# A gated Fourier and Mish kernel: its hand-paced schedule is replaced by a list of operations sorted by when the matmul engine wants each

## The chip, the core and the metric

The kernel runs on one core of one Trainium2 chip. The metric is device microseconds of one execution, the median of timed runs. A core has the matmul engine TensorE (PE, with its weight loads PEld), VectorE (DVE), ScalarE (ACT), GpSimd (POOL) and SyncE (SP). Matmuls add into eight PSUM banks of 128 x 512 floats; ACT and DVE copy or add them out into SBUF tiles. DMAs carry tiles between SBUF and DRAM. Each engine works off its own queue in order, and instructions wait on semaphores.

## The reference

```python
x = A_x                                                  # 1 x 2048 x 640
g = sigmoid((x * gate_w).sum(-1, keepdims=True))
a = x @ dft_hid_re.T;  b = x @ dft_hid_im.T
A = dft_seq_re @ a - dft_seq_im @ b                      # Fourier mixing
h = x @ w1 + b1                                          # 640 -> 1728
B = (h * tanh(softplus(h))) @ w2                         # Mish, 1728 -> 640
out = g * A + (1 - g) * B
```

All is float32.

## The kernel before, in words

**Products.** Each float32 operand is split into a high part in PE's float32r format (a copy on ACT) and the rest (a subtraction on DVE): `split`, line 82. A product of two operands is three matmuls, `mm3` (line 91): high x high, high x low, low x high, each 128 x 128 weights by 128 x 512 columns.

**Stages.** Work is cut into tiles of 512 of the 2048 positions, two tiles to a "problem" (class `Problem`, line 293). Four problems multiply the sequence matrices by x (stage seq, results u), two multiply u by the hidden matrices (hid, results y), the dense part takes x by w1 and Mish (results act), and two problems take act by w2 and add y (out). u, y and act pass through DRAM scratch. Each problem is a 2 x 2 block product with seven products in place of eight (Winograd's form): sums and differences of the moving tiles (`s1` to `s4`) are made on DVE before their splits, and those of the weight blocks on DVE in jobs (`low`, `w1_job`). The 640 columns are four such blocks and a fifth, "block 5", that is multiplied plainly.

**Turns in a problem.** `first()` multiplies tile 11 by `a` (two banks) and by block 5 (`d1`). `second()` (line 343) goes through turns "22", "21", "s2", "s1"; "21" exists for block 5 of the second tile alone (`d2`, line 357). `third()` (line 452) goes through "12", "s3", "s4".

**The dense stage.** `dense_rest` does the columns of w1 that don't pair up. `dense_first` (line 734) goes through six blocks of w1 for each half of the positions. A block is eight steps on four banks (lines 863 to 870): a11 on bank a, s1 on b, d2 on d, s2 on a, s4 and d1 on b, s3 on a, a12 and d1 on c, a22 and d2 on a. Between two products on one bank, what it holds is copied out (`snap`) or added out (`add`).

**What sets the order.** `steps` (line 113) is the order of PE. The loop at lines 1040 to 1087 goes through it: for the step LEAD (7, or 6) ahead it issues the loads and splits; then the step's matmuls; then stores that are three steps old (`stores`, line 116, issued on SP); then what follows the step. Jobs (weight splits, the gate, products by g and 1 - g) start when a running sum of DVE's work is below that of PE (line 1079). All loads and stores are on SP's queue.

**The gate.** For each of four tiles, `gate` (line 885) multiplies five tiles of transposed x by columns of gate_w, splits the sum and multiplies it by a matrix of ones: two matmuls. g and 1 - g go to scratch as whole tiles. `gate_y` (line 919) loads each y again, multiplies it by g and stores it: 20 times.

**Buffers.** 20 tiles of 512 columns (f), 4 of 640 (fx), 10 operand pairs (rh, rl), 26 weight pairs of 640 columns (wh, wl).

Of the kernel before, what the change touches and what calls it, by code (L numbers as in the profile page):

```python
# [13 lines left out]
P = 128  # L14
# [8 lines left out]
LEAD = 7  # L23
LEAD_D = 6
AHEAD = 9
SPARE, SPARE_D, SPARE_OUT = 3, 5, 4
SLACK, SLACK_UP = -1.0, 2.5
NR, NFS, NFX, NW, NL = 10, 20, 4, 26, 4
MM = 0.2267


class Slots:


    def __init__(self, items):
        self.free = list(items)

    def get(self):
        return self.free.pop(0)

    def put(self, *items):
        self.free.extend(items)
# [3 lines left out]
def fnet_mish_gate(ctx: ExitStack, tc: tile.TileContext, xn, xt, c_re, c_im, wd_re, wd_im,  # L46
# [7 lines left out]
    psum = Slots([pp.tile([P, N], F32, name=f"ps{i}") for i in range(8)])  # L54
    R = Slots([(sb.tile([P, N], F32R, name=f"rh{i}"), sb.tile([P, N], F32R, name=f"rl{i}")) for i in range(NR)])
    FS = Slots([sb.tile([P, N], F32, name=f"f{i}") for i in range(NFS)])
    FX = Slots([sb.tile([P, D], F32, name=f"fx{i}") for i in range(NFX)])
    W = Slots([(sb.tile([P, D], F32R, name=f"wh{i}"), sb.tile([P, D], F32R, name=f"wl{i}")) for i in range(NW)])
    ones = sb.tile([P, P], F32R, name="ones")
    b1s = sb.tile([P, NF], F32, name="b1s")  # L60
    gws = sb.tile([P, KD], F32, name="gws")

    def scratch(name, n, rows=P):
        return [[dr.tile([rows, N], F32, name=f"{name}{i}_{t}") for t in range(TG)] for i in range(n)]

    usc, ysc = scratch("u", 2 * KD), scratch("y", KD)
    gsc, qsc = scratch("g", 1)[0], scratch("q", 1)[0]
    asc = scratch("act", FC) + [[dr.tile([FR, N], F32, name=f"actr_{t}") for t in range(TG)]]

    clock = {"pe": 0.0, "dve": 0.0, "step": 0}  # L70
# [4 lines left out]
    def tt(o, a, b, op):  # L75
        clock["dve"] += 0.14 + 0.54 * a.shape[-1] / N
        nc.vector.tensor_tensor(o, a, b, op=op)  # L77

    def copy(o, a, scale=1.0):
        nc.scalar.activation(o, a, AF.Copy, scale=scale)  # L80

    def split(h, l, src):

        copy(h, src)
        tt(l, src, f32(h), OP.subtract)

    def mm(ps, a, b, start, stop):
        clock["pe"] += MM
        nc.tensor.matmul(ps, a, b, start=start, stop=stop, skip_group_check=True)  # L89

    def mm3(ps, ah, al, bh, bl, start, stop):
        mm(ps, ah, bh, start, False)
        mm(ps, ah, bl, False, False)
        mm(ps, al, bh, False, stop)

    def part(w, a, b):
        return w[0][:, a:b], w[1][:, a:b]

    def blocks(w, at, n):
        return [part(w, at + j * P, at + (j + 1) * P) for j in range(n)]  # L100

    A2, B2 = slice(0, 2 * P), slice(2 * P, 4 * P)

    RAW, XS, PS, OPS, KEEP, X, H = {}, {}, {}, {}, {}, {}, {}
    steps, stores, events, attach, narrow, takes = [], [], {}, [], set(), {}

    def at(i, fn):

        events.setdefault(i, []).append(fn)

    def step(raw, preps, mms, post=None):
        steps.append([list(raw), list(preps), mms, post])

    def store(dst, v, f):
        stores.append((dst, v, f, clock["step"] + (3 if clock["step"] < len(steps) - 8 else 0)))


    jobs, loaded, running, done_jobs = [], [], [], set()  # L120

    class Job:
        def __init__(self, key, work, load=lambda: [], w=0, fx=0, fs=0):
            self.key, self.work, self.load, self.w, self.fx, self.fs = key, work, load, w, fx, fs

    def simple(fn):
        def work(*a):
            fn(*a)
            return
            yield  # L130
        return work

    def fx_load(src, width=D):
        f = FX.get()
        nc.sync.dma_start(f if width == D else f[:, :width], src)
        return f

    def fs_load(src):
        f = FS.get()
        nc.sync.dma_start(f[:src.shape[0]], src)  # L140
        return f

    def job_load(i):
        j = jobs.pop(0)
        loaded.append((j, j.load(), i))

    def job_start():
        j, a, _ = loaded.pop(0)
        running.append((j.key, j.work(*a)))

    def job_go():
        key, work = running[0]
        pause = next(work, None)
        if pause is None:
            running.pop()
            done_jobs.add(key)
        return pause or 0

    def need(key):
        while key not in done_jobs:  # L160
            if not running:
                if not loaded:
                    job_load(0)
                job_start()
            job_go()

    class Stage:  # L170


        def __init__(self, kind, kh, row, neg=False):
            self.kind, self.kh, self.row, self.neg = kind, kh, row, neg
            self.XA, self.XB, self.XT13 = [None] * kh, [None] * kh, [None] * kh
            self.XT2 = [None] * (kh // KD + 1)

    def t2_part(st, k):
        return part(st.XT2[k // KD], k % KD * P, (k % KD + 1) * P)

    def b_sums(f, g):

        t = FS.get()
        tt(f[:, A2], f[:, B2], f[:, A2], OP.subtract)
        tt(f[:, B2], g[:, B2], f[:, B2], OP.subtract)
        tt(t[:, A2], g[:, B2], f[:, A2], OP.subtract)
        tt(t[:, B2], g[:, A2], t[:, A2], OP.subtract)
        return t

    def top(st, k, a, five):  # L190
        w = st.XA[k] = st.XA[k] or W.get()
        split(*part(w, 0, 2 * P), a)
        split(*part(w, 2 * P, 3 * P), five)

    def low(st, k, g, f):
        if st.neg:
            copy(g, g, -1.0)
            yield 1
        t = b_sums(f, g)
        yield 0  # L200
        w = st.XB[k] = W.get()
        st.XA[k] = st.XA[k] or W.get()
        st.XT13[k] = W.get()
        if k % KD == 0:
            st.XT2[k // KD] = W.get()
        split(*w, g)
        FX.put(g)
        yield 0
        split(*part(st.XA[k], 3 * P, 5 * P), t[:, B2])
        split(*part(st.XT13[k], 4 * P, 5 * P), t[:, :P])  # L210
        split(*t2_part(st, k), t[:, P:2 * P])
        FS.put(t)
        yield 0
        split(*part(st.XT13[k], 0, 4 * P), f)
        FS.put(f)

    tops = set()

    def stage_jobs(st, order):
        def do_top(k, g):  # L220
            top(st, k, g[:, A2], g[:, 4 * P:])
            FX.put(g)

        for what, k in order:
            if what == "top":
                jobs.append(Job((st.kind, "top", k), simple(lambda g, k=k: do_top(k, g)),
                                lambda k=k: [fx_load(st.row(k))], (st.kind, k) not in tops, 1))
            else:
                jobs.append(Job((st.kind, "low", k), lambda g, f, k=k: low(st, k, g, f),
                                lambda k=k: [fx_load(st.row(k + st.kh)), fs_load(st.row(k)[:, :4 * P])],  # L230
                                2 + (k % KD == 0) + ((st.kind, k) not in tops), 1, 1))
            tops.add((st.kind, k))

    def c_split(key, f):
        r = OPS[key] = R.get()
        split(r[0], r[1], f)
        FS.put(f)

    def op_done(key):
        R.put(OPS.pop(key))  # L240

    def product(name, stationary, key, first, last):

        if first and name not in PS:
            PS[name] = [psum.get() for _ in stationary]
        for ps, w in zip(PS[name], stationary):
            mm3(ps, *w, *OPS[key], first, last)

    def products_by_part(uses, key):

        h, l = OPS[key]
        todo = []
        for name, stationary in uses:
            PS[name] = [psum.get() for _ in stationary]
            todo += zip(PS[name], stationary)
        for n, c in ((0, h), (0, l), (1, h)):
            for ps, w in todo:
                mm(ps, w[n], c, n == 0 and c is h, False)

    def free_banks(name):  # L260
        psum.put(*PS.pop(name))

    def copy_out(name, keep=False):
        f = [FS.get() for _ in PS[name]]
        for ps, o in zip(PS[name], f):
            copy(o, ps)
            if not keep:
                psum.put(ps)
        if not keep:
            PS.pop(name)  # L270
        return f

    def add_out(name, f, keep=False):

        for ps, a in zip(PS[name], f):
            tt(a, ps, a, OP.add)
        if not keep:
            free_banks(name)
        return f
# [853 lines left out]
```

## Time and profile before

| what | value |
|---|---|
| three timed runs | 885.54, 885.94, 887.34 us |
| median | 885.94 us |
| span of the profiled execution | 882.2 us |
| PE busy, matmuls | 864.0 us, 3780 |
| DVE busy, instructions | 724.2 us, 1262 |
| ACT busy, instructions | 477.5 us, 909 |
| DMA bytes, mean rate | 217.32 MB, 246 GB/s |

The span runs from the first to the last instruction of one execution; the median lies 3.7 us above it, and the time of that execution apart from its span isn't recorded. Of the 3780 matmuls 8 warm PE up and 8 belong to the gate; 3764 are the products: 1728 in seq, 540 in hid, 100 in the dense rest, 648 in the dense blocks, 748 in out. A row of the profile names the engine, the line, the operation, and out<-in by tile: ps is a bank, f and fx are plain tiles, rh and rl the parts of a moving operand, wh and wl those of a weight. Matmul spans overlap, so their number times the pace says more than the busy time.

### The profile page before, as it was taken

How to read it: one execution, taken by the hardware profiler on the slowest of the kernel's cores; microseconds unless marked ns; L12 is line 12 of the kernel's file. 1: busy time of each engine (PE TensorE's matmuls, PEld its weight loads, DVE VectorE, ACT ScalarE, POOL GpSimd, SP SyncE). 2: the span in 40 equal slices, each digit the busy share in tenths (PEclk: the TensorE clock that was granted, in tenths of full speed). 3: DMA queues.
4: the chain of work that ended last, by engine and by line, in shares of the span. 5: the costliest groups of instructions: out<-in, count | busy, mean ns of one | idle time of the engine just before them, and what ended most of it. 6: DMA issues, size and time to landing. Idle time of an engine off the chain costs nothing.

```text
span 882.2 us, 12203 instructions
## 1 busy us (share of the span) xinstructions
PE 864.0 (98%) x3780; PEld 710.4 (81%) x3780; DVE 724.2 (82%) x1262; ACT 477.5 (54%) x909; POOL 0.2 (0%) x4
## 2 busy tenths in 40 slices
PE   8999999999999999999999999899899999999998
PEld 6888888888888888888888888687688788888886
DVE  5999987899799668998997987663875889798994
ACT  6756545454565545647665667543644656442442
POOL 0000000000000000000000000000000000000000
PEclk9999999999999999999999999999999999999999
DMA  9975759596889664768767795489676777394952
GB/s 323 328 236 175 245 185 324 164 312 235 302 275 351 202 221 156 259 226 283 265 236 273 247 316 178 138 308 367 204 256 214 268 260 240 133 330 142 367 203 107
DMA packets 119392, 217.32 MB, mean 246 GB/s; under 512 B 13600, under 2 KB 16032, under 8 KB 119328
## 3 DMA queue, kind: packets, MB, share of 16 engines
q1 hardware_dynamic: 119184, 216.43, 71.6%
q8 instruction: 29, 0.48, 0.2%
q14 instruction: 35, 0.29, 0.1%
q10 hardware_dynamic: 144, 0.13, 0.0%
HBM read 170.11 MB, written 46.40 MB: 245 GB/s over the span
## 4 chain that ended last, share of the span: by engine, by line
PE 93%; DVE 3%; ACT 1%; DMA 1%; issue 1%; SPq 0%; DVEq 0%; ACTq 0%
PE ps L89 93%; DVE f L77 1%; DVE wl L77 1%; ACT wh L80 1%; DMA y<-f 1%; DVE rl L77 0%; DMA f<-in_xn_dram 0%; ACT f L671 0%; DMA act<-f 0%; DVE fx L77 0%; ACT f L80 0%; ACT rh L80 0%; SPq L1031 0%; SPq L1051 0%; DVE f L477 0%
## 5 line engine op out<-in xcount | busy, mean ns | idle before, releaser
L89 PE MATMUL ps<-rh,wh 128*128 128x512 f32 x1067 | 415.7, 390 | 7.4 <-ACT f L80 3.4
L89 PE MATMUL ps<-rh,wl 128*128 128x512 f32 x1053 | 409.4, 389 | 0.0
L89 PE MATMUL ps<-rl,wh 128*128 128x512 f32 x1052 | 409.1, 389 | 0.0
L80 ACT ACTIVATE rh<-f 128x512 fp32r<-128x512 f32 x413 | 243.7, 624 | 158.3 <-DVE f L77 103.9
L77 DVE TENSOR_TENSOR rl<-f,rh 128x512 fp32r<-128x512 f32 x411 | 267.0, 685 | 47.7 <-ACT rh L80 47.0
L89 PEld LDWEIGHTS ps<-rh,wh 128*128 128x128 f32 x1067 | 200.4, 188 | 52.7 <-ACT f L80 5.0
L89 PEld LDWEIGHTS ps<-rh,wl 128*128 128x128 f32 x1053 | 197.7, 188 | 40.9
L89 PEld LDWEIGHTS ps<-rl,wh 128*128 128x128 f32 x1052 | 197.4, 188 | 40.9 <-DVE rl L77 0.2
L77 DVE TENSOR_TENSOR f<-f,f 128x512 f32<-128x512 f32 x303 | 207.0, 689 | 19.2 <-DMA u<-f 6.3
L80 ACT ACTIVATE f<-ps 128x512 f32<-128x512 f32 (+1 forms) x146 | 84.9, 593 | 92.7 <-PE ps L89 74.7
L80 ACT ACTIVATE wh<-f 128x512 fp32r<-128x512 f32 (+2 forms) x158 | 68.9, 475 | 49.4 <-DVE f L77 40.4
L77 DVE TENSOR_TENSOR f<-ps,f 128x512 f32<-128x512 f32 x90 | 59.0, 685 | 35.1 <-PE ps L89 35.1
L77 DVE TENSOR_TENSOR wl<-f,wh 128x512 fp32r<-128x512 f32 (+2 forms) x157 | 73.8, 502 | 16.2 <-ACT wh L80 16.0
L89 PE MATMUL ps<-wh,wh 128*128 128x512 f32 x201 | 79.3, 395 | 5.4 <-ACT f L80 2.8
L89 PE MATMUL ps<-wl,wh 128*128 128x512 f32 x196 | 77.0, 393 | 0.0
L89 PE MATMUL ps<-wh,wl 128*128 128x512 f32 x195 | 76.6, 393 | 0.0
L77 DVE TENSOR_TENSOR wl<-fx,wh 128x640 fp32r<-128x640 f32 (+3 forms) x82 | 43.7, 554 | 11.6 <-ACT wh L80 11.6
L671 ACT ACTIVATE f<-f,b1s 128x512 f32<-128x512 f32 x36 | 25.9, 721 | 49.2 <-DVE f L77 49.2
L89 PEld LDWEIGHTS ps<-wh,wh 128*128 128x128 f32 x201 | 38.0, 189 | 15.4 <-ACT f L80 4.2
L80 ACT ACTIVATE wh<-fx 128x128 fp32r<-128x128 f32 (+5 forms) x83 | 40.6, 514 | 10.5 <-DMA fx<-in_xn_dram 3.5
L89 PEld LDWEIGHTS ps<-wh,wl 128*128 128x128 f32 x195 | 37.0, 190 | 7.8
L89 PEld LDWEIGHTS ps<-wl,wh 128*128 128x128 f32 x196 | 37.1, 189 | 7.5
(43 smaller groups left out, 177.3 us busy)
## 6 DMA issues: line engine op xcount, KB each, us to landing
f<-in_c_re_dram SPq DMA_DIRECT2D x128, 256.0 KB, 4.2
f<-in_c_im_dram SPq DMA_DIRECT2D x128, 256.0 KB, 4.1
f<-act SPq DMA_DIRECT2D x84, 256.0 KB, 5.2
f<-u SPq DMA_DIRECT2D x80, 256.0 KB, 4.6
f<-in_xt_dram SPq DMA_DIRECT2D x64, 256.0 KB, 4.6
act<-f SPq DMA_DIRECT2D x54, 256.0 KB, 4.5
u<-f SPq DMA_DIRECT2D x40, 256.0 KB, 3.5
y<-f SPq DMA_DIRECT2D x40, 256.0 KB, 4.5
```

Source lines behind the costliest of these rows:

```text
L77: nc.vector.tensor_tensor(o, a, b, op=op)
L80: nc.scalar.activation(o, a, AF.Copy, scale=scale)
L89: nc.tensor.matmul(ps, a, b, start=start, stop=stop, skip_group_check=True)
L671: nc.scalar.activation(o[rows], src[rows], AF.Mish, bias=b1s[rows, f:f + 1])
```

## The change

The arithmetic helpers stay; what orders them is new. Every operation is put into a list (`Graph.add`) in program order with its engine, the tiles it reads and writes, and an assumed duration. PE's operations keep their order, one every 0.2267 us. From this `wants()` works out backwards when each other operation must begin. `run()` then plays the engines through: each free engine takes, of the operations whose inputs are done, the one with the earliest want, if tiles are free beyond those that more urgent operations will ask for. The order that comes out is what is emitted on each queue. The real waits stay semaphores.

```diff
-LEAD = 7
-SLACK, SLACK_UP = -1.0, 2.5
-NR, NFS, NFX, NW, NL = 10, 20, 4, 26, 4
+NR, NFS, NX, NW = 10, 18, 6, 26
+HOP, PROMPT, LATER, AHEAD = 0.15, 2.0, 8.0, 5.0
+    def wants(self):
+        for op in self.ops:
...
+            if op.engine == "PE":
+                op.ends = op.at + op.took
+                op.want = op.at
+                continue
...
+        for op in reversed(self.ops):
+            late = min([a.want for a in op.after], default=1e9) - op.took - HOP
+            op.want = late if op.want is None else min(op.want, late)
```

*Block 5.* Turn "21" is gone. `second()` begins with a copy of `d1`'s result into the bank of `d2`, and block 5 is multiplied by s3 (21 less 11) in `third()`:

```diff
-            for p, k in in_turn(kh, ("22", "21", "s2", "s1"), ("22", "21", "s2", "s1"), ("22", "21", "s2", "s1")):
+            self.d2 = copy(bank(), d2)
+            for p, k in in_turn(kh, *[("22", "s2", "s1")] * 3):
...
+                elif p == "s3":
+                    product(self.a, st.blocks("t3", k), x, False, end)
+                    product([self.d2], st.blocks("five", k), x, False, end)
```

*Turns of the dense blocks.* Two blocks of w1 go together, on all eight banks:

```diff
-        for fp in range(FP):
-            step([], [...], sub(fp, [("a", "a11", at_cols(0, 0), True, True)]), p1_post)
-            step([], [], sub(fp, [("b", "s1", at_cols(2, 0), True, True)]), p5_post)
-            step([], [], sub(fp, [], [("d", "d2", 1, True, True)]))
-            step([], [], sub(fp, [("a", "s2", t2_at(fp), False, True)]), p6_post)
+        for f0 in range(0, FP, 2):
+            pair_ = (f0, f0 + 1)
+            bk = {f: [bank() for _ in range(4)] for f in pair_}
+            for f in pair_:
+                times(bk[f][0], "a11", [(w[f][0], k) for k in range(2)], True, True)
+                p1[f] = to_sbuf(bk[f][0])
+            for f in pair_:
+                times(bk[f][1], "s1", [(w[f][2], k) for k in range(2)], True, True)
+                p5[f] = to_sbuf(bk[f][1])
+            for f in pair_:
+                times(bk[f][3], "d2", [(w[f][1], 4)], True, True)
+            for f in pair_:
+                times(bk[f][0], "s2", [(w[f][2], 4), (T2B[f // KD], f % KD)], False, True)
+                u2[f] = to_sbuf(bk[f][0])
```

*The gate.* Rows of x (128 positions by 640) times the broadcast gate_w, summed along the row by one DVE instruction each; the 16 columns of g and of 1 - g are stored to DRAM as rows of 2048 floats and loaded back with each 512 of them broadcast to 128 partitions. y is multiplied by g as it leaves the banks of hid.

```diff
-        mm(ps, ones, r[0], True, False)
-        mm(ps, ones, r[1], False, True)
+            dve(lambda k=k, x=x: nc.vector.scalar_tensor_tensor(
+                x.t, x.t, 1.0, wide.t, op0=OP.mult, op1=OP.mult, accum_out=gcol.t[:, k:k + 1]),
...
+            dma("SP", lambda c=c, row=row: nc.sync.dma_start(row.t.rearrange("o (k p) -> p (o k)", p=P), c.t),
+    def broadcast(row, t):
+        return load(FS, lambda: row.t[:, t * N:(t + 1) * N].partition_broadcast(P), row)
```

*Stores.* All stores to DRAM scratch are issued by GpSimd; those of the output stay on SP.

```diff
-            nc.sync.dma_start(dst, v)
+    ISSUE = {"SP": nc.sync, "POOL": nc.gpsimd}
+    STORES = "POOL"
```

*Ends.* The first loads are the c tile, the x tile and then the column loads of block 5; warm-up uses a part of an operand tile in place of the matrix of ones, which needs a second memset. The end of the last product is as before.

More of the change, by code (lines that the diff above doesn't have):

```diff
@@ L79, in copy @@
-    def copy(o, a, scale=1.0):
[L80 to L97, printed above, removed]
@@ L138, in fs_load @@
[L138 to L165, printed above, removed]
@@ L234, in c_split @@
[L234 to L258, printed above, removed]
@@ L281, in preload, with whole, dve, act @@
-    def preload(name, f):
-        PS[name] = [psum.get() for _ in f]
-        for ps, a in zip(PS[name], f):
-            copy(ps, a)
+    def whole(*vals):
+        return [(v, None) for v in vals]
+    def dve(emit, r, w, n=N, more=0.0):
+        took = 0.15 + n / 960 + more
+        return G.add("DVE", emit, r, w, took, took - 0.083)
+    def act(emit, r, w, n=N, more=0.0):
+        took = 0.21 + n / 1260 + more
+        return G.add("ACT", emit, r, w, took, took - 0.096)
+    def dma(queue, emit, r, w, size):
+        return G.add(queue, emit, r, w, 1.95 + size / 385e3, 0.605 if queue == "SP" else 1.0)
@@ new lines, in tt, with fresh, to_sbuf @@
+    def tt(o, a, b, op, cut=(slice(None),) * 3, rows=slice(None), n=N):
+        (x, y, z) = cut
+        dve(lambda: nc.vector.tensor_tensor(o.t[rows, x], a.t[rows, y], b.t[rows, z], op=op),
+            whole(a, b), whole(o), n)
+    def fresh(pool, a, b, op):
+        o = Val(pool)
+        tt(o, a, b, op)
+        return o
+    def copy(o, a, scale=1.0):
+        act(lambda: nc.scalar.activation(o.t, a.t, AF.Copy, scale=scale), whole(a), whole(o))
+        return o
+    def to_sbuf(bank):
+        return copy(Val(FS), bank)
@@ new lines, in split, with operand @@
+    def split(w, at, src, a=0, n=N):
+        c = slice(at * P, at * P + n)
+        s = slice(a, a + n)
+        ks = range(at, at + n // P)
+        hs, ls = [(w, (k, 0)) for k in ks], [(w, (k, 1)) for k in ks]
+        act(lambda: nc.scalar.activation(w.t[0][:, c], src.t[:, s], AF.Copy), whole(src), hs, n)
+        dve(lambda: nc.vector.tensor_tensor(w.t[1][:, c], src.t[:, s], f32(w.t[0][:, c]), op=OP.subtract),
+            whole(src) + hs, ls, n)
+    def operand(src, pool=None):
+        r = Val(pool or R)
+        act(lambda: nc.scalar.activation(r.t[0][:, :N], src.t[:, :N], AF.Copy), whole(src), [(r, 0)])
+        dve(lambda: nc.vector.tensor_tensor(r.t[1][:, :N], src.t[:, :N], f32(r.t[0][:, :N]), op=OP.subtract),
+            whole(src) + [(r, 0)], [(r, 1)])
+        return r
@@ new lines, in mm, with mm3, product @@
+    def mm(bank, w, k, wn, x, xn_, start, stop):
+        G.add("PE", lambda: nc.tensor.matmul(bank.t, w.t[wn][:, k * P:k * P + P], x.t[xn_][:, :N], start, stop,
+                                             skip_group_check=True),
+              [(w, (k, wn)), (x, xn_)], whole(bank), 0.42)
+    def mm3(bank, b, x, start, stop):
+        w, k = b
+        mm(bank, w, k, 0, x, 0, start, False)
+        mm(bank, w, k, 0, x, 1, False, False)
+        mm(bank, w, k, 1, x, 0, False, stop)
+    def product(banks, blocks, x, start, stop):
+        for bank, b in zip(banks, blocks):
+            mm3(bank, b, x, start, stop)
@@ new lines, in first @@
+                top(k)
+                x = operand(self.moving(self.t1, k))
+                banks, blocks = self.a + [self.d1], st.blocks("b11", k) + st.blocks("five", k)
+                if not G.pe:
+                    for n, c in ((0, 0), (0, 1), (1, 0)):
+                        for b, (w, j) in zip(banks, blocks):
+                            mm(b, w, j, n, x, c, n == 0 and c == 0, False)
+                else:
+                    product(banks, blocks, x, k == 0, k == kh - 1)
+            self.p1, self.d = [to_sbuf(b) for b in self.a], to_sbuf(self.d1)
@@ new lines, in done, with plus @@
+        def done(self, b, d, t):
+            f = Val(FS)
+            if self.q:
+                tt(f, b, self.q(t), OP.mult)
+            else:
+                copy(f, b)
+            self.plus(f, d, t)
+        def give(self, d, t, f):
+            if self.q:
+                tt(f, f, self.q(t), OP.mult)
+            self.plus(f, d, t)
+        def plus(self, f, d, t):
+            if self.st is fin and not self.y:
+                tt(f, f, load_of(FS, ysc[d][t]), OP.add)
+            self.finish(d, t, f)
@@ new lines, in end, with emit, send @@
+        def end(self):
+            (p0, p1), t, h = self.b, self.t1, N // 2
+            f, g = Val(FS), Val(FS)
+            copy(f, p0)
+            self.finish(2, t, f, "SP")
+            for eng, c in (("ACT", slice(0, h)), ("DVE", slice(h, N))):
+                def emit(c=c, eng=eng):
+                    if eng == "ACT":
+                        nc.scalar.activation(g.t[:, c], p1.t[:, c], AF.Copy)
+                    else:
+                        nc.vector.tensor_copy(g.t[:, c], p1.t[:, c])
+                (act if eng == "ACT" else dve)(emit, whole(p1), [(g, eng)], h)
+                def send(c=c, eng=eng):
+                    o = out[3 * P:4 * P, t * N + c.start:t * N + c.stop]
+                    (nc.scalar if eng == "ACT" else nc.sync).dma_start(o, g.t[:, c])
+                G.add("ACT" if eng == "ACT" else "SP", send, [(g, eng)], [], 2.3, 0.1)
@@ new lines, in w1_rest, with cut @@
+    def w1_rest():
+        if W1C:
+            return
+        W1C.append(Val(W))
+        split(W1C[0], 0, load(X, w1a[FC - 1], cols=D), 0, D)
+        g, w = load(X, w1b, cols=KD * FR), Val(W)
+        W1R.append(w)
+        ks = [(w, (k, 0)) for k in range(KD)]
+        def cut(t, n):
+            return t[:, :KD * n].rearrange("p (k f) -> p k f", k=KD)
+        act(lambda: nc.scalar.activation(cut(w.t[0], P)[:, :, :FR], cut(g.t, FR), AF.Copy), whole(g), ks, KD * FR)
+        dve(lambda: nc.vector.tensor_tensor(cut(w.t[0], P)[:, :, FR:], cut(g.t, FR), f32(cut(w.t[0], P)[:, :, :FR]),
+                                            op=OP.subtract), whole(g) + ks, ks, KD * FR)
@@ new lines, in w2_rest @@
+    def w2_rest():
+        if W2C:
+            return
+        W2C["c"], W2C["r"] = Val(W), Val(W)
+        split(W2C["c"], 0, load(X, w2[(FC - 1) * P:FC * P], cols=D), 0, D)
+        g = Val(X)
+        for i in range(2):
+            dma("SP", lambda i=i: nc.sync.dma_start(g.t[i * FR:i * FR + FR], w2[FC * P:]), [], [(g, i)], FR * D * 4)
+        w = W2C["r"]
+        hs, ls = [(w, (k, 0)) for k in range(KD)], [(w, (k, 1)) for k in range(KD)]
+        gs = [(g, 0), (g, 1)]
+        act(lambda: nc.scalar.activation(w.t[0], g.t, AF.Copy), gs, hs, D)
+        dve(lambda: nc.vector.tensor_tensor(w.t[1], g.t, f32(w.t[0]), op=OP.subtract), gs + hs, ls, D)
@@ new lines, in out_act, with dense_rest @@
+    def out_act(f, t, o, src, rows=P, bias=True):
+        mish(o, src, f, slice(0, rows), bias)
+        if t >= 2:
+            q = keep(("qx", t, f >= FC - 1), lambda: broadcast(qrow, t))
+            tt(o, o, q, OP.mult, rows=slice(0, rows))
+        store(asc[f][t], o, rows)
+    def dense_rest(t, xs):
+        w1_rest()
+        c = bank()
+        for k, x in enumerate(xs):
+            mm3(c, (W1C[0], k), x, k == 0, k == KD - 1)
+        out_act(FC - 1, t, Val(FS), c)
+        r = bank()
+        for k, x in enumerate(xs):
+            mm(r, W1R[0], k, 0, x, 0, k == 0, False)
+            mm(r, W1R[0], k, 0, x, 1, False, k == KD - 1)
+        a, b, q = Val(FS), Val(FS), slice(0, FR)
+        act(lambda: nc.scalar.activation(b.t[q], r.t[FR:], AF.Copy), whole(r), whole(b))
+        dve(lambda: nc.vector.scalar_tensor_tensor(a.t[q], r.t[q], b1s.t[q, FC:], b.t[q], op0=OP.add, op1=OP.add),
+            whole(r, b, b1s), whole(a), more=0.06)
+        out_act(FC, t, a, a, FR, False)
@@ new lines, in out_rest @@
+    def out_rest(t, banks, cols, opened):
+        w2_rest()
+        c, r, f = operand(load_of(FS, asc[FC - 1][t])), Val(R), load_of(FS, asc[FC][t], FR)
+        act(lambda: nc.scalar.activation(r.t[0][:FR, :N], f.t[:FR], AF.Copy), whole(f), [(r, 0)])
+        dve(lambda: nc.vector.tensor_tensor(r.t[0][FR:, :N], f.t[:FR], f32(r.t[0])[:FR, :N], op=OP.subtract),
+            whole(f) + [(r, 0)], [(r, 0)])
+        for i, (b, e) in enumerate(zip(banks, cols)):
+            mm3(b, (W2C["c"], e), c, i < opened, False)
+            mm(b, W2C["r"], e, 0, r, 0, False, False)
+            mm(b, W2C["r"], e, 1, r, 0, False, True)
@@ L1088, in fnet_mish_gate @@
-    for dst, v, f, _ in stores:
-        nc.sync.dma_start(dst, v)
-        FS.put(f)
+    hd[0].first(hid.top)
+    hd[1].first(hid.top)
+    for p in hd:
+        p.second(hid.low)
+        p.third()
+    for t in (2, 3):
+        dense_rest(t, [operand(raw(t, k)) for k in range(KD)])
+    have = {}
+    for t, names in ((0, ("a11", "a11", "a12", "a12", "d1")), (1, ("a21", "a21", "a22", "a22", "d2"))):
+        xs = [operand(raw(t, k), W if n in ("a11", "a12", "a22") else R) for k, n in enumerate(names)]
+        for k, n in enumerate(names):
+            if n != "a21":
+                have[n, k % 2 if k < 4 else 0] = xs[k]
+        dense_rest(t, xs)
@@ L1093 @@
+    dense_first(0, have)
+    dense_first(1, {})
+    ou[0].first(fin.top)
+    ou[1].first(fin.top)
+    for p in ou:
+        p.second(fin.low)
+        p.third()
+    G.run([psum, R, FS, X, W], 385.0, 1.95)
 def kernel(**inputs):
```

1221 lines of the change are left out of this document (445 added, 776 removed).

## The prediction

> **What bounds the kernel now.** I read the page first: its span, and the chain that ended last.
>
> ```profile
> span 882.2 us, 12203 instructions
> ...
> PE 93%; DVE 3%; ACT 1%; DMA 1%; issue 1%; SPq 0%; DVEq 0%; ACTq 0%
> ```
>
> PE is the chain. What there is to win is PE's idle time, its count of matmuls, and the two ends. The windows view, cut where the chain leaves PE (554.5 us) and comes back for good (706.3 us), tells where PE idles; (x) is the number of instructions.
>
> ```profile
> core 0: us, PE busy (x) PEld busy (x) DVE busy (x) ACT busy (x) POOL busy (x), PEclk, DMA share, GB/s
> 7.40:554.50 547.10, 547.10 (x2413) 453.02 (x2414) 472.36 (x818) 320.14 (x608) 0.00 (x0) 1.00 0.74 252
> 554.50:706.30 151.80, 140.96 (x604) 112.97 (x603) 103.97 (x197) 76.70 (x151) 0.00 (x0) 0.99 0.75 256
> 706.30:878.50 172.20, 172.14 (x757) 141.89 (x757) 146.18 (x243) 77.91 (x147) 0.00 (x0) 1.00 0.65 224
> ```
>
> The first row gives the pace: 547.10 / 2413 = 0.2267 us a matmul at a granted clock of 1.00. The third keeps it (757 x 0.2267 = 171.6 of 172.2). The second doesn't: 604 x 0.2267 = 136.9 of 151.8, so 14.9 us are lost in the 648 matmuls of the first dense layer. DVE is busy there for 104 of 152 us and ACT for 77: neither is full, so the loss is one of order. The waits view of the weight loads (PE's front) names it; the columns are us in total, times, longest.
>
> ```profile
> PEld ps L89 <- ACT f L80: 9.2, 10, 2.8
> PEld ps L89 <- DVE f L77: 6.3, 4, 1.8
> ```
>
> Fourteen waits, 15.5 us, all for a copy or an add that empties a bank that PE wants again. Queried for the window alone, the view gives the same two rows. One of them in the timeline (start, us):
>
> ```profile
> 563.73 0.42 ACT L80 ACTIVATE wh<-f 128x256 fp32r<-128x256 f32 x1 [1.44 <-DVE f L77]
> ...
> 564.36 0.58 ACT L80 ACTIVATE f<-ps 128x512 f32<-128x512 f32 x1
> ...
> 564.99 0.50 PE L89 MATMUL ps<-rh,wh 128*128 128x512 f32 x1 [1.62 <-ACT f L80]
> ```
>
> The copy out of the bank (f<-ps) stands in ACT's queue behind the splitting of a w1 block (wh<-f), which itself waited 1.44 us for DVE's sums; PE waits 1.62 us. In the code a block's step leaves 9 matmuls (2.04 us) between the last matmul on a bank and the next on the same bank (s1 and d2 between a11 and s2, and so on).
>
> **The change, part by part.** Rows for the prices (busy us, mean ns):
>
> ```profile
> L77 DVE TENSOR_TENSOR rl<-f,rh 128x512 fp32r<-128x512 f32 x411 | 267.0, 685 | 47.7 <-ACT rh L80 47.0
> L80 ACT ACTIVATE rh<-f 128x512 fp32r<-128x512 f32 x413 | 243.7, 624 | 158.3 <-DVE f L77 103.9 <-PE ps L89 39.8 <-DMA f<-act 4.9
> ...
> L80 ACT ACTIVATE f<-ps 128x512 f32<-128x512 f32 (+1 forms) x146 | 84.9, 593 | 92.7 <-PE ps L89 74.7 <-DMA y<-f 6.7 <-DVE rl L77 3.8
> ...
> L80 ACT ACTIVATE ps<-f 128x512 f32<-128x512 f32 x26 | 14.5, 596 | 1.9 <-DVE f L77 1.9
> L894 DVE SCALAR_TENSOR_TENSOR f<-f,gws,f 128x512 f32<-128x512 f32 x16 | 11.9, 745 | 0.0
> ```
>
> *Pairs of blocks.* The turns of two blocks now alternate (a11, a11, s1, s1, d2, d2, ...). The new order of PE's instructions has 24 matmuls between two products on one bank: 5.44 us. Of this 0.39 goes for the last matmul and 0.59 for the copy, leaving 4.4 us, against 1.0 before. The longest wait above was 2.8 us beyond that 1.0, so 3.8 us of delay were the worst; 4.4 cover them. ACT's and DVE's queues are also sorted by when PE wants each. Gain 15.5 us; bounds 0 and 15.5. I take 14.5, leaving 1.0, because blocks are still split in the stage.
>
> *Block 5.* The operand "21" goes: 4 x 8 + 2 x 5 + 2 x 6 = 54 splits, 54 x 0.685 = 37.0 us of DVE and 54 x 0.624 = 33.7 of ACT; eight preloads come (8 x 0.596 = 4.8 us of ACT). The matmuls stay (three a turn move from "21" to "s3"). All lies beside PE: nothing in the sum. One preload is exposed: in the fourth sequence problem, second() starts right after first(), and only 6 matmuls (1.36 us) stand between the last matmul on d1 and the first on d2. They need 0.39 + 0.59 (out) + 0.60 (in) = 1.6, and up to two more copies ahead in ACT's queue (1.2): a wait of 0.2 to 1.5; I take 0.6.
>
> *Gates.* The 8 matmuls with ones go: 8 x 0.2267 = 1.8 us of PE. In their place 16 products of 640 columns on DVE (estimate by columns from the 512-column row: 16 x 0.745 x 640/512 = 14.9 us for 16 x 0.745 = 11.9), a sigmoid and a subtraction of 16 columns, two column stores and ten broadcast loads. The 20 multiplications of y by g move into the end of the hidden stage, where 12 of them replace ACT copies; 20 stores and 20 loads of y go. Beside PE: nothing, except for the column stores (rivals).
>
> *Stores by GpSimd.* 128 stores leave SP's queue (829 issues before, 643 after). SP then no longer holds loads behind a store that isn't ready. No load is among the waits above, so this gains nothing. What it costs POOL the trace doesn't show; nearest are SP's issue of three stores (timeline) and the landing of a 256 KB store (DMA view):
>
> ```profile
> 737.59 1.42 SPq L1060 DMA_DIRECT2D po<-f  x3
> ```
>
> ```profile
> act<-f SPq DMA_DIRECT2D x54, 256.0 KB, 4.5
> ```
>
> So 0.47 to 4.5 us for each on POOL. The densest place is the dense stage: 8 stores per pair of blocks, in 108 x 0.2267 = 24.5 us, or 3.06 us each. Below that POOL keeps up. I take 1 us, near the issue row since several stores are in flight (eight semaphores in turn), and cost it at nothing. The Trainium skill ("DMA: Bandwidth & Descriptors", Anatomy of one DMA — SWDGE (gpsimd) path) gives about 2.0 us plus bytes / 436e3 for a store issued there, an estimate of 2.6 us for 256 KB; even if POOL were held for all of it, by that the sum would be the same.
>
> *The start.* Rows (start, us):
>
> ```profile
> 1.58 3.78 PE L89 MATMUL ps<-rh,ones 128*128 128x512 f32 x8 [1.58 <-DVE rh L940]
> 1.78 0.48 SPq L1051 DMA_DIRECT2D f<-in_c_re_dram  x1
> 2.30 0.43 SPq L1051 DMA_DIRECT2D f<-in_xn_dram  x1
> ...
> 6.21 0.42 ACT L80 ACTIVATE wh<-f 128x256 fp32r<-128x256 f32 x1 [4.20 <-DMA f<-in_xn_dram]
> ...
> 7.40 0.96 PE L89 MATMUL ps<-rh,wh 128*128 128x512 f32 x3 [2.03 <-ACT rh L80]
> ```
>
> Before, two loads of columns 512 to 639 went out ahead of these, and the x tile, fourth, ended the wait. After, the c tile, the x tile and one column load go first, so the last transfer needed is third (an issue earlier, 0.5 us), and the second column load (3 x 128 x 128 floats) no longer shares the wires with it. Warm-up sets the floor: one more memset (0.48), so 1.58 + 0.48 + 3.78 = 5.84. I take 6.1 for 7.4: gain 1.3, bounds 0 and 1.6.
>
> *The end of the last product* is cut the same way, so the tail stays:
>
> ```profile
> 878.05 0.39 PE L89 MATMUL ps<-rh,wl 128*128 128x512 f32 x1
> 878.48 0.38 ACT L80 ACTIVATE f<-ps 128x256 f32<-128x256 f32 x1 [0.76 <-PE ps L89]
> 878.89 0.37 ACTq L475 DMA_DIRECT2D out_dram<-f  x1
> ```
>
> From the last matmul's start to the end of the span: 882.2 - 878.05 = 4.15.
>
> *What is late next.* With dense waits gone, PE reaches the last layer 15 us sooner relative to DVE. At its entry, ACT's queue copies ou[1].first's three banks behind w2 splits that wait for DVE, and 13 matmuls (2.9 us) later PE wants the first of these banks: 1.2 us of copies and 0.4 of the last matmul, plus up to 3.8 of delay like that above: 0 to 2.5, I take 0.8. At ou[1].second, DVE has 24 operations in its queue from the first product of the emptied banks to the split that PE needs (24 x 0.685 = 16.4 us) against 63 matmuls (14.3): 0 (they overlap) to 2.2 us, I take 1.2.
>
> Sum: 6.1 + 3763 x 0.2267 (853.1) + 4.15 = 863.3; waits 1.0 + 0.6 + 0.8 + 1.2 = 3.6; span 866.9. The same sum for the kernel before (7.4 + 3771 x 0.2267 + 4.15 + 15.5) gives 881.9 for 882.2, so 0.3 is missing: 867.2. The profiled execution's span lies 3.7 under the median of the three timed runs (885.94): 870.9.
>
> **The rivals.**
>
> *The dense waits stay.* If a copy out of a bank is still stuck behind more than 4.4 us of splits, 24 matmuls don't cover it. All fourteen waits kept: 870.9 - 1.0 + 15.5 = 885.4, no change; half of them: 877.7. For it: blocks are split in the stage as before. Against: the worst delay seen was 3.8.
>
> *The column stores block SP.* Each of the two writes 2048 pieces of 4 bytes, 128 per DMA engine, and the broadcast of the first row waits for it at the head of SP's queue.
>
> ```profile
> q1 hardware_dynamic: 119184, 216.43, 71.6%
> ```
>
> A packet took 0.716 x 882.2 x 16 / 119184 = 0.085 us. If a 4-byte piece costs as much, a store takes 10.9 us plus some 2: 9 more than a tile's 4 us, with SP halted. The hidden stage uses three loads in 21 matmuls (4.8 us); if half of the 18 tiles hold loads ahead, that covers 14 us. Without cover: 879.9. The Trainium skill ("DMA: Bandwidth & Descriptors", Specifications) speaks against such stores: under 512 B a transfer doesn't run at line rate but is read, modified and written. No row here shows one; by that rule this rival is no rarity.
>
> *POOL becomes the bound (slower).* If POOL is held until a store has landed (4.5 us), the 48 stores of the first dense layer take 216 us for 147 of PE: 870.9 + 69 = 940. It decides from 3.06 us, and the kernel is slower than before from 3.06 + (887.7 - 870.9) / 48 = 3.4 us a store. For it: POOL issued nothing before, so nothing excludes it. Against: the issue row, and the stores' separate semaphores.
>
> **How the numbers follow.** Forecast, 866.5 to 875: 0.70. Dense waits stay in part or whole, 875 to 886: 0.13 (0.03 of it no change). Column stores, around 880: 0.07. POOL bound, above 888: 0.10. Low end of the range: no wait left and the floor at the start, 5.84 + 853.1 + 4.15 + 0.3 + 3.7 = 867.1, and 0.6 for the runs' spread. The high end, 882, holds half the dense waits or the blocked queue. Faster by over 0.2% (about what a measurement of this kernel can tell): 0.87; within: 0.03; slower: 0.10.
>
> **What would show it.** PE's row with 8 fewer matmuls; weight loads waiting for ACT f and DVE f in the dense stage under 2 us in all; first real matmul near 6.1; PE idle at the fourth sequence problem's second() and at both entries of the last layer, under 4 us together; POOL's issues near 1 us. I am wrong if the dense window still holds over 5 us of waits, if SP halts behind grow with PE waiting for u loads, or if POOL's stores follow one another without a gap while tiles run out.

## The result, and the profile after

The changed kernel takes **882.84 us** (median of seven runs, 881.37 to 884.84) where the kernel before took 886.48 beside it (883.74 to 888.07): a ratio of 0.9963, 95% interval 0.9953 to 0.9974. It is faster by 0.37%; 1.7% was forecast. The profiled run took 882.19 us with a span of 880.4, so 1.8 us lie around the span.

The windows view of the changed kernel, cut at its own stages (end of seq at 415, end of hid near 540, dense blocks 555 to 706):

```profile
7.10:415.00 407.90, 407.56 (x1798) 336.93 (x1797) 324.74 (x576) 224.04 (x414) 24.85 (x46) 1.00 0.69 241
415.00:481.00 66.00, 55.70 (x246) 45.83 (x245) 52.87 (x100) 28.54 (x51) 2.56 (x5) 0.95 0.79 244
481.00:555.00 74.00, 74.00 (x319) 61.09 (x320) 71.95 (x135) 45.73 (x91) 12.51 (x24) 0.97 0.85 305
555.00:706.00 151.00, 151.00 (x668) 125.08 (x667) 99.38 (x188) 89.92 (x166) 27.59 (x51) 1.00 0.53 183
706.00:792.00 86.00, 86.00 (x381) 71.21 (x381) 60.08 (x104) 40.12 (x72) 1.64 (x4) 1.00 0.62 212
792.00:822.00 30.00, 27.79 (x119) 21.83 (x118) 26.07 (x43) 8.22 (x14) 0.00 (x0) 1.00 0.73 257
```

Multiply each count by 0.2267. The dense stage, which lost 14.9 us before, loses nothing (668 x 0.2267 = 151.4 of 151.0). The loss is now elsewhere: 66.00 - 55.8 = 10.2 us in the second row, 74.00 - 72.3 = 1.7 in the third (granted clock 0.97), 30.00 - 27.0 = 3.0 in the last. The waits of PE, whole run (us, times, longest), hold the first of these in one row:

```profile
PE ps L292 <- DVE f L259: 10.3, 1, 10.3
PE ps L292 <- ACT ps L268: 2.2, 3, 1.5
```

The chain of the stretch before it (start us, us, what) shows what DVE waited for: u tiles that took 12 and 13 us to come, and behind the last of them 9.7 us of sums, splits and additions out of banks until PE can go on.

```profile
442.77 12.22 DMA f<-u
...
457.44 0.37 SPq L753
...
457.86 13.29 DMA f<-u
...
477.60 3.09 DVE f L259 x5
480.69 0.14 issue
```

SP's timeline of that stretch: L753 is the column stores, L246 the loads. An issue took 0.37 or 0.38 us on rows such as 442.10 and 449.40; right behind the first column store two single issues take 3.80 and 2.69, and behind the second one three loads span 5.62.

```profile
442.10 0.37 SPq L753 DMA_DIRECT2D grow<-gcol  x1
442.77 3.80 SPq L246 DMA_DIRECT2D f<-u  x1
446.62 2.69 SPq L246 DMA_DIRECT2D x<-in_w1a_dram  x1
449.40 0.38 SPq L246 DMA_DIRECT2D f<-u  x1
454.03 0.80 SPq L246 DMA_DIRECT2D f<-grow  x2
...
457.44 0.37 SPq L753 DMA_DIRECT2D qrow<-qcol  x1
457.86 5.62 SPq L246 DMA_DIRECT2D f<-u  x3
463.57 0.86 SPq L246 DMA_DIRECT2D f<-ph  x2
```

And the DMA view of 435 to 481 us (size each, median us from issue to landing): 8 KB need twice as long as 256 KB, and u's loads 7.3 where their median over the run is 5.7.

```profile
f<-u SPq DMA_DIRECT2D x19, 256.0 KB, 7.3
...
grow<-gcol SPq DMA_DIRECT2D x1, 8.0 KB, 11.9
qrow<-qcol SPq DMA_DIRECT2D x1, 8.0 KB, 11.1
```

So the theory to test: the forecast was right but for the two column stores, 2048 pieces of 4 bytes each, which hold up the loads behind them. The plan itself counts each of them as 256 KB (`1 << 18` in the code), which by its formula is 2.6 us.

### The profile page after: what moved, and what is told of

Same layout as the page of the kernel before. It is cut to its first block, busy times and chain, and to the rows that moved or that the text cites. A ratio compares the mean times of both kernels' runs of the same rounds, so it can differ in the third digit from the quotient of the medians.

```text
span 880.4 us, 11973 instructions
## 1 busy us (share of the span) xinstructions
PE 861.5 (98%) x3772; PEld 710.2 (81%) x3772; DVE 677.8 (77%) x1213; ACT 461.6 (52%) x849; POOL 69.3 (8%) x132
## 4 chain that ended last, share of the span: by engine, by line
PE 85%; DMA 6%; DVE 6%; ACT 1%; issue 1%; SPq 0%; ACTq 0%; DVEq 0%
PE ps L292 85%; DMA f<-u 4%; DVE f L259 3%; DMA x<-in_xn_dram 1%; DMA f<-po 1%; DVE x L746 1%; DVE x L259 0%; DVE r8l L287 0%; ACT f L268 0%; DVE r9l L287 0%; DMA out_dram<-f 0%; ACT r8h L286 0%; DVE r1l L287 0%; DVE r5l L287 0%; ACT r1h L286 0%
## 5 line engine op out<-in xcount | busy, mean ns | idle before, releaser
L268 ACT ACTIVATE f<-ps 128x512 f32<-128x512 f32 x129 | 74.5, 595 | 40.2 <-PE ps L292 35.1
L286 ACT ACTIVATE r9h<-f 128x512 fp32r<-128x512 f32 x42 | 26.4, 629 | 23.1 <-PE ps L292 10.7
L255 POOL DMA_DIRECT2D act<-f x52 | 28.2, 542 | 131.0 <-DVE f L259 65.3
L287 DVE TENSOR_TENSOR r3l<-f,r3h 128x512 fp32r<-128x512 f32 x41 | 28.2, 688 | 11.6 <-ACT r3h L286 11.2
L287 DVE TENSOR_TENSOR r9l<-f,r9h 128x512 fp32r<-128x512 f32 x42 | 28.9, 688 | 9.6 <-ACT r9h L286 9.0
L287 DVE TENSOR_TENSOR r0l<-f,r0h 128x512 fp32r<-128x512 f32 x40 | 27.5, 688 | 11.4 <-ACT r0h L286 11.3
L287 DVE TENSOR_TENSOR r2l<-f,r2h 128x512 fp32r<-128x512 f32 x41 | 28.2, 688 | 10.0 <-ACT r2h L286 9.7
L287 DVE TENSOR_TENSOR r8l<-f,r8h 128x512 fp32r<-128x512 f32 x39 | 26.8, 688 | 11.3 <-ACT r8h L286 11.0
L287 DVE TENSOR_TENSOR r6l<-f,r6h 128x512 fp32r<-128x512 f32 x40 | 27.5, 688 | 9.7 <-ACT r6h L286 9.4
L287 DVE TENSOR_TENSOR r5l<-f,r5h 128x512 fp32r<-128x512 f32 x40 | 27.5, 688 | 9.2 <-ACT r5h L286 8.9
```

Source lines behind the costliest of these rows:

```text
L255: dma(queue, lambda: ISSUE[queue].dma_start(d.t, v.t[:rows]), whole(v), whole(d), rows * N * 4)
L268: act(lambda: nc.scalar.activation(o.t, a.t, AF.Copy, scale=scale), whole(a), whole(o))
L286: act(lambda: nc.scalar.activation(r.t[0][:, :N], src.t[:, :N], AF.Copy), whole(src), [(r, 0)])
L287: dve(lambda: nc.vector.tensor_tensor(r.t[1][:, :N], src.t[:, :N], f32(r.t[0][:, :N]), op=OP.subtract), whole(src) + [(r, 0)], [(r, 1)])
```

## The experiments

Each kernel was timed beside the kernel before on the same chip. The median of the latter lay between 886.5 and 887.6 on the chips used, so differences between kernels from different chips are good to about 1 us.

### Column stores in 64-byte pieces

```diff
-            x = load(X, xn[k], cols=D)
+            x = load(X, xn.rearrange("a b d -> (a b) d").rearrange("(p k) d -> k p d", k=KS)[k], cols=D)
...
-            nc.sync.dma_start(row.t.rearrange("o (k p) -> p (o k)", p=P), c.t)
+            nc.sync.dma_start(row.t.rearrange("o (p k) -> p (o k)", p=P), c.t)
```

> The x tiles of the gates hold other tokens (partition p of tile k holds token 16p+k instead of 128k+p), so that each column store is 128 pieces of 64 B instead of 2048 pieces of 4 B; every instruction keeps its place in the order. Theory (the 4-byte pieces of the two column stores jam the DMA rings of SP's queue, u's loads behind them land late, PE idles 10.3 us near 470 and then runs at a lower clock for 1.7 us): both stores land in 2 to 3 us, PE's idle row of 10.3 us is gone, the time falls by 10 to 12 us to 871 to 873. Rival A (SP's own halt for the broadcast of grow, a queue wait that stays whatever the store looks like): 880 to 883, with the idle row still over 8 us. Rival B (u's stores through GpSimd come too late for u's loads): 880 to 883 likewise, with the stores landing in 3 us.

Measured: **869.82 us** (869.28 to 869.89), ratio 0.9804 (0.979 to 0.9819): 13.0 under the changed kernel, a little more than the theory's 10 to 12. Each queue moves the same bytes as before, SP's in 3840 packets fewer. Its window rows for the two stretches, and its DMA rows for 435 to 481 us:

```profile
415.00:481.00 66.00, 66.00 (x293) 54.66 (x292) 64.13 (x119) 33.75 (x59) 6.97 (x13) 1.00 0.88 316
481.00:555.00 74.00, 74.00 (x328) 61.29 (x327) 73.82 (x142) 52.01 (x104) 9.77 (x18) 1.00 0.75 269
```

```profile
f<-u SPq DMA_DIRECT2D x32, 256.0 KB, 5.3
...
grow<-gcol SPq DMA_DIRECT2D x1, 8.0 KB, 5.0
qrow<-qcol SPq DMA_DIRECT2D x1, 8.0 KB, 1.4
```

293 matmuls where there were 246, and the clock at 1.00. The same 8 KB land in 5.0 and 1.4 us where they took 11.9 and 11.1, and the three loads behind the second store span 1.37 us. The time rules out both rivals.

### One store at a time

Edit: as above, but one of the two stores keeps `"o (k p) -> p (o k)"`. The x tiles are those of the 64-byte pieces, so one row holds its values at other tokens, and only the time is read.

> As e1_rows16, but the store of qrow keeps its 2048 pieces of 4 B (that of grow has 128 pieces of 64 B). The x tiles are those of e1_rows16, so that the values of qrow stand at other tokens. Theory: the two jams of about 11 us each add up against a cover of some 12 us of f tiles loaded ahead; one alone is nearly covered, so the time is 871 to 874, and neither this run nor e3 shows half of the loss. Rival A (each store costs PE its own share): half of the loss here, 876 to 877. Rival B (the second store, right in front of u's last loads for the fourth problem of the hidden stage, is the one that counts): 880 to 883 here and 871 to 873 in e3.

> As e1_rows16, but the store of grow keeps its 2048 pieces of 4 B (that of qrow has 128 pieces of 64 B). The values of grow stand at other tokens. Theory: one jam nearly covered, 871 to 874. Rival A (each store its own share): 876 to 877. Rival B (the qrow store alone): 871 to 873. Rival C (SP's queue halt for the landing of grow, 4 us, plus the loads behind it): 880 to 883 here and 871 to 873 in e2.

Measured: qrow alone **878.82** (877.94 to 881.56), grow alone **877.14** (875.4 to 877.68): 9.0 and 7.3 above 869.82. Rival A (each its own share) is nearest, though both times lie above its 876 to 877, and my expectation of a covered jam was wrong. PE's wait in each (qrow alone, then grow alone):

```profile
PE ps L292 <- DVE f L259: 7.1, 1, 7.1
```

```profile
PE ps L292 <- DVE f L259: 5.2, 1, 5.2
```

The scattered store lands in 12.8 us (qrow; 1.4 with 64-byte pieces) or 12.5 (grow; 5.0). Between 435 and 481 us DVE then waits 9.8 or 7.9 us for u tiles, where it waited 1.7 with 64-byte pieces and 12.9 in the changed kernel. 7.1 or 5.2 us of that reach PE. The rest of the loss is PE's clock, as the windows after the wait show (grow alone: the idle stretch, the first matmuls, what follows):

```profile
471.00:476.20 5.20, 0.00 (x0) 0.00 (x0) 5.20 (x10) 2.96 (x6) 0.75 (x2) 0.71 0.35 101
476.24:480.20 3.96, 3.96 (x10) 3.16 (x11) 3.96 (x7) 0.60 (x1) 2.71 (x6) 0.53 0.84 277
480.20:490.00 9.80, 9.80 (x45) 8.10 (x44) 9.08 (x16) 5.08 (x9) 1.87 (x4) 1.00 1.02 379
```

Ten matmuls in 3.96 us at a granted clock of 0.53: 1.7 us more than at full pace. Both stores together cost 13.0, not 9.0 + 7.3 = 16.3: the delays partly overlap.

### The stores on another queue

Edit: `nc.scalar.dma_start` for `nc.sync.dma_start` in the column stores.

> The changed kernel with both column stores (2048 pieces of 4 B each) issued by ACT instead of SP, in the same place of the order. If the jam is in SP's queue (loads issued behind the store on the same queue have to stand behind its pieces), the loads overtake it here and the time is 871 to 875. If the jam is in the 16 DMA engines themselves, whatever queue the pieces come from, the loads are late as before and the time stays at 879 to 883. I hold the engines for the likelier, 0.6 to 0.4. [...]

Measured: **880.49** (875.05 to 884.66, a wide spread; ratio 0.9889 to 0.9965). The stores land in 14.2 and 16.9 us, and PE still waits 7.8 us in one piece for DVE's f. SP waits 11.5 us for grow, and this halt alone would hold up the loads behind it. But two loads of u that SP issued right behind the stores (which ACT issued at 441.44 and 459.23, in 0.38 and 0.37 us), and so outside that halt, land late as well (chain):

```profile
441.64 11.10 DMA f<-u
...
459.59 11.28 DMA f<-u
```

That is 11 us, where the median with 64-byte pieces was 5.3 and the chain of the changed kernel had 12.22 and 13.29. So the delay comes mostly from what the two queues share, not from the order of one. The Trainium skill ("DMA: Bandwidth & Descriptors", Issuing engines are not separate DMA queues) says that DMAs of all issuing engines run on the same sixteen DMA engines; this run agrees.

### Pieces of 16 bytes

Edit: x tiles and rows so that each store is 512 pieces of 16 B (`"o (a p b) -> p (o a) b"`, a = b = 4).

> As e1_rows16, but each column store is 512 pieces of 16 B (the x tiles hold tokens so that the rows come out right). Theory (the price goes with the number of pieces, about 5 ns each beside 2 us: 11 us for 2048): landing 4.5 us, PE's idle row near 470 under 1 us, time 869.5 to 871. Rival (the price belongs to pieces under some length between 16 and 64 B, whatever their number): landing near 11 us and 879 to 883.

Measured: **869.9** (869.18 to 870.94); the stores land in 5.8 (behind loads) and 3.2 us (quiet). Over the landings of qrow, with few loads under way, 128, 512 and 2048 pieces took 1.4, 3.2 and 11.1 us: (11.1 - 3.2) / 1536 = 5.1 ns a piece, or 82 ns on each of 16 engines. The price goes with the number of pieces. The rule of the Trainium skill that the prediction cited ("DMA: Bandwidth & Descriptors", Specifications) speaks of lengths under 512 B; pieces of 16 and 64 B fall under it too and cost nothing that shows in the kernel's time here.

### What took the dense waits away

First, on the kernel with 64-byte pieces (869.82), single blocks instead of pairs (`for f0 in range(FP): pair_ = (f0,)`):

> On e1_rows16 (869.8 us): the dense layer's blocks run one after the other instead of in pairs, each with its own four banks; the sorted queues and everything else stay. Theory (the pairs took the 15.5 us of dense waits away, by putting twice as many matmuls between a bank's last product and the next one into it): most of them come back, 880 to 886. Rival (the order of ACT's and DVE's queues by want did it, the pairs only come on top): 870 to 873. I hold the pairs for the likelier, 0.55 to 0.45.

Measured: **872.5** (872.03 to 872.59), only 2.7 more. Then the lines of ACT and DVE in the dense stage in order of readiness instead of by want, with pairs and with single blocks:

```diff
-                        insort(ready[a.engine], (a.want, a.n))
+                        insort(ready[a.engine], (now + 5.0 if a.engine in ("ACT", "DVE") and a.n in self.plain else a.want, a.n))
```

> On e1_rows16 (869.8 us): in the two calls of the first dense layer, ACT and DVE take their operations in the order in which they become ready, instead of sorted by when PE wants the result; pairs stay. Theory (new, after e5_single_blocks gave back only 2.7 us: the sorted lines of ACT and DVE took most of the 15.5 us away, and either cure alone nearly does it): 870 to 873. Rival (sorting is what is needed, pairs don't help without it): 878 to 886.

> On e5_single_blocks (872.5 us): ACT and DVE take the dense layer's operations in the order in which they become ready, with single blocks, so that both cures are off. Theory (two cures for the same waits): 880 to 888, with 8 us or more of PE idle in the dense stage. Rival (neither matters, the waits of the kernel before came from something else in its plan, such as its stores on SP or its extra splits): 872 to 875.

Measured: **880.07** (879.21 to 883.96) and **883.04** (882.7 to 884.86). In time, sorting is worth 10 us and pairs about 3, whichever way the other stands. But bank waits aren't where these 10 us lie. With pairs unsorted, PE's waits in the dense stage are all for splits of operands (1.9, 1.4, 1.2, 0.7 and 0.5 us), none for a bank. With both off, the weight loads' waits for a bank in the dense stage are these:

```profile
PEld ps L292 <- ACT f L268: 2.8, 1, 2.8
PEld ps L292 <- DVE f L259: 0.7, 1, 0.7
```

That is 3.5 us, not the 15.5 of the kernel before. And the windows of the pairs unsorted put the loss ahead of most of the blocks: 2.8 us from 481 to 530 (204 matmuls in 49 us), still in the hidden stage, 6.9 from 545 to 580 (124 in 35), at the dense blocks' entry, and none from 580 to 706 (557 in 126). Unsorted lines make operands late, which the kernel before didn't do. So this edit isn't the kernel before in that respect, and the plain test is the other way round: pairs alone in the kernel before, its lines still paced by hand (edit: its eight steps for two blocks in turn, with banks and copies per block).

> The kernel before with one edit: the eight steps of a dense block go in pairs of blocks, on eight banks, in the same order of PE as in the changed kernel. Its planner, splits, gate and stores stay. Theory as the prediction put it (24 matmuls between two products on a bank cover every delay of a copy): the bank waits of 15.5 us go, 870 to 874. Rival (the hand-paced lines of ACT and DVE are the cause, as single blocks with sorted lines lost only 2.7 us): under half of it goes, 879 to 887. I hold the theory for the likelier, 0.6, as pairs with unsorted lines (e9) showed no wait for a bank in the dense stage.

Measured: **882.83** (880.79 to 885.3, 12 runs), ratio 0.9957 (0.9942 to 0.9972). By the time the rival wins, but the waits tell it apart. The weight loads' waits in the dense stage:

```profile
PEld ps L89 <- DVE f L77: 3.3, 2, 2.5
PEld ps L89 <- ACT f L80: 1.0, 1, 1.0
```

15.5 us have become 4.3: pairs do cover most bank waits, as the prediction had it. But the kernel gains 3.9, not 11. The gain is given back at the entry of the last layer (a row of PE's waits there, and the chain):

```profile
PE ps L89 <- ACT f L80: 4.9, 1, 4.9
```

```profile
713.92 5.17 DMA act<-f
719.09 0.02 issue
719.11 5.32 DMA f<-act
```

A tile of act is loaded right behind its store, which on SP's queue has only just been issued. DVE waits for it, ACT's splits wait for DVE, and a copy out of a bank stands behind them. PE, now earlier, waits 4.9 us for that copy, then runs at 0.50 for 4 us (9 matmuls, 2.0 us more than at full pace). It is the kind of wait that the prediction's *What is late next* put at this entry.

### Who issues the stores

On the kernel with 64-byte pieces: `STORES = "SP"`, then `OUTS = "POOL"`, then the stores of out on ACT.

> On e1_rows16 (869.8 us): the scratch stores are issued by SP, as in the kernel before, instead of GpSimd. Theory (SP's line halts at a store until its data is there, and the loads behind it go out late): 872 to 880, with PE waits for f<-u or f<-act loads. Rival (the loads stand far enough ahead, GpSimd bought nothing): 869 to 870.5.

> On e1_rows16 (869.8 us): the stores of out (but for the last ones) are issued by GpSimd as well. Theory (the 2 us lost at the entry of the last layer's second problem come from loads held behind stores of out on SP): 867.5 to 868.5. Rival (PE waits there for ACT to copy the banks' first values, not for loads): 869.4 to 870.2.

> On e1_rows16 (869.8 us): the stores of out in the last layer are issued by ACT instead of SP. Theory (loads of act for the last problem stand on SP behind stores of out that wait for DVE): the 2 us of PE waits near 808 fall under 1 us, 868.5 to 869.3. Rival (loads wait for tiles that stores of out still read, whoever issues them, as GpSimd's stores showed): 869.5 to 871.

Measured: **873.51** (871.79 to 877.92), **872.37** (871.45 to 873.17), **871.84** (871.51 to 873.01). Scratch stores on GpSimd are worth about 3.7 us by the medians; the single runs of the first lie 2 to 8 us above 869.82. The 2.8 us left at the last layer's second problem don't go by moving its output stores; both moves cost 2 to 2.6. A wait for tiles that those stores still read fits this, but what would take it away wasn't found.

## Why the prediction was wrong

The step that failed is "Beside PE: nothing, except for the column stores (rivals)": the sum held the column stores at nothing, since the rival put a cover of 14 us against them. They cost 13.0. Their price was about right: 10.9 plus 2 us a store estimated, 11.1 to 11.9 measured, and 85 ns a piece on an engine estimated, 82 measured. The rival's time, 879.9, is 3 us from the result; it was given 0.07.

The cover was the error: 18 tiles, half of them loads ahead, were taken as 14 us between load and matmul. But PE doesn't wait for a tile there. It waits for a bank, which DVE empties by an addition (f<-ps), and this addition stands in DVE's queue behind the sums of the late u tiles. The same operations in the changed kernel and then with 64-byte pieces (timeline):

```profile
479.99 1.28 DVE L259 TENSOR_TENSOR f<-ps,f 128x512 f32<-128x512 f32 x2
480.82 0.76 PE L292 MATMUL ps<-r4h,w11h 128*128 128x512 f32 x1 [10.30 <-DVE f L259]
```

```profile
466.83 1.28 DVE L259 TENSOR_TENSOR f<-ps,f 128x512 f32<-128x512 f32 x2
470.52 0.39 PE L292 MATMUL ps<-r4h,w11h 128*128 128x512 f32 x1
```

Undisturbed, the first of the two additions ends at 466.83 + 0.68 = 467.5, and PE wants the bank at 470.5. The cover was 3.0 us. The late tiles put DVE's queue back by 479.99 - 466.83 = 13.2 us, and 13.2 less 3.0 is PE's wait of 10.3 but for 0.1. It holds with one store too: qrow alone puts the additions back by 11.0 us (477.85) and grow alone by 8.6 (475.41), for waits of 7.1 and 5.2; PE itself came 0.9 and 0.3 us later there. Nor could DVE catch up: with 64-byte pieces it is busy for 64.13 of the 66 us and 73.82 of the 74 in its two window rows above. In the kernel before it was 58.85 and 61.81 in the same stretches.

What covered PE was the time that DVE was ahead of it, not the number of tiles. The range's high end, 882, missed by 0.8: the rival left out the second store's share and the 1.9 us at half clock.

Point by point, with 869.82 (the kernel without that step's loss) for the sum:

- **Sum and ends.** Span 867.2 forecast, 868.0 measured there. The 3.7 us around the span were the difference of a profiled run and a median; within one run it is 1.8 for the changed kernel and 2.2 to 2.5 for the kernel before.
- **Pairs.** Size right: 15.5 us gone, 14.5 taken. Cause half right: in the kernel before, pairs alone remove 11.2 of them, but don't bring the time, since the last layer's loads then come late. In the new kernel single blocks have 2.6 us of bank waits, and 3.5 with the lines unsorted, so there the waits are mostly gone without pairs and without sorting. What else in the new order removes them stays open.
- **Block 5.** Hidden, as said: DVE's busy time fell from 724.2 to 677.8 us. The exposed preload held the weight loads 0.76 us (0.6 taken).
- **Gates.** 3780 matmuls became 3772, as said.
- **Stores by GpSimd.** 0.54 us each on POOL, inside the bounds of 0.47 to 4.5 and under the 3.06 that decides. "This gains nothing" was wrong: on the new plan they are worth about 3.7 us.
- **The start.** 6.1 taken. The first product begins at 5.58 us, but the third waits until 6.74 for the split of block 5's column load. By the pace, 1801 matmuls before 415 us (1798 and the three before 7.1) and 0.3 of waits give 415 - 408.3 - 0.3 = 6.4: a gain of 1.0, not 1.3.
- **The last layer.** The first entry lost nothing (0.8 taken: 381 matmuls in 86.0 us); the second 3.0 (1.2 taken, bounds 0 to 2.2).

## What to carry to other kernels

Count the pieces of a DMA, not its bytes: a store that scatters single floats costs the time of many tiles on all queues, and a layout that leaves each partition one contiguous run removes it. Tiles loaded ahead don't say how late a load may come: an engine between load and matmul works in order, and what PE needs of it can stand behind the late tile. So read the cover from when that engine is done to when PE wants the result, and ask whether the engine has time to catch up. A stage that gets faster moves its consumers' loads closer to their stores: check what is late next there.

## What was not expected of the hardware

The end of a wait isn't the end of its cost. After 4.9, 5.2, 7.1, 7.8 and 10.3 us of idle PE (five kernels) the granted clock stood at 0.50 to 0.57 for the next 4 us, and matmuls came 0.43 us apart, 8 to 14 of them: 1.7 to 2.9 us more each time. The changed kernel, from the end of its wait:

```profile
480.82:484.77 3.95, 3.94 (x9) 3.11 (x10) 3.95 (x7) 0.60 (x1) 2.70 (x6) 0.51 0.79 281
484.77:500.00 15.23, 15.23 (x68) 12.58 (x67) 13.18 (x23) 7.12 (x13) 1.89 (x4) 1.00 1.03 376
```

The Trainium skill ("TensorE: Matmul & The Clock Gate", What's actually happening) says that an idle window of about 3.4 us halves the clock and a busy one restores it; the rows of these long waits agree. But a shorter wait was enough in the kernel before: after 2.39 us, the longest bank wait there, 10 matmuls took 3.79 us at 0.55, 1.5 us more than at full pace. After 2.09 us, with pairs in the kernel before, the clock stayed at 1.00. So waits under the page's figure can cost the clock too.

And SP is itself held behind a store of many small pieces: one issue took 3.80 us right behind 2048 pieces of 4 bytes, and 0.32 behind 128 pieces of 64.
